# One build-time plan for gating, token mixing and the first channel chunk, with another matmul order

## The chip, the cores and the metric

The kernel runs on one core of one Trainium2 chip. The metric is the device time of one launch in microseconds (us), as the median of repeated runs. The engines are PE (TensorE, matmuls; PEld is its weight load), DVE (VectorE), ACT (ScalarE), POOL (GpSimd) and SP (SyncE, which here only issues DMAs). Each engine works through its own queue in program order.

## The reference

```python
attn_out = _attn_ref(q, k, v)            # 4 batches, 8 heads, 1152 keys, 576 pooled queries, 64 wide
x = attn_out.transpose(0, 2, 1, 3).reshape(4, 576, 512)
# gating (_moe_ref)
h = gelu(x @ w_in)                       # 512 -> 1024
u, v = h[..., :512], h[..., 512:]
v_n = (v - mean(v)) / sqrt(var(v) + 1e-6) * g_ln
v_s = einsum('ts,bsd->btd', w_sg, v_n) + b_sg[None, :, None]      # w_sg is 576 x 576
x = x + (u * v_s) @ w_out
# token mixing, then channel mixing (_moe2_ref)
u = x + (relu(x.T @ w_tok1) @ w_tok2).T  # 576 -> 256 -> 576 along tokens
out = u + relu(u @ w_ch1) @ w_ch2        # 512 -> 1536 -> 512
```

All weights arrive as 64-bit floats and are turned into pairs of 32-bit floats on the chip.

## The kernel before

Every matmul operand is held as a high and a low float32r part, and each product is three matmul passes (high by high, low by high, high by low). The state `xT` (channels on partitions, 2304 tokens) stays in SBUF through all stages.

Attention lays out its work with the class `Plan`: tasks with an engine, a duration, dependencies, rings of buffers and an urgency. `Plan.run` emits each engine's tasks in the order that this model gives; PE's order is written out in `line()`. Its last few tasks (the final part of the last head pair) are kept back in `rest` and emitted inside the next stage.

Gating, in `spatial`, runs batch by batch (b = 0 to 3). One batch is: V, five row tiles of `x @ w_in` for the v half (`v_mm`, L1001; four in odd batches, whose 64-row tail shares a tile with the batch before); O, the output product of the batch before (`wo_mm`, L1108, four tiles); U, four tiles of the u half (`u_mm`, L1067); S, four tiles of the product with `w_sg` (`sg_mm`, L1084). V and U results go through a gelu of two ACT and two DVE steps (L937 to L944). V is then normalised (L1014 to L1045) and split: the high part by ACT (L1051), the low part by POOL (`sub`, L241, tile `vn`). S results pass DVE (L1093), POOL (L1096), ACT (L1098) and DVE (L241, tile `g`) before O can read them. The input of the next batch is split by ACT (`x_high`, L399) and POOL (`x_low`, L241, tile `x`). V tiles of one pair, U, S and three of the four O tiles share three PSUM buffers (`ps2`).

Token mixing, in `mixing`, comes when the last O is done. For each batch: Y, five transposed tiles (`y_tr`, L1249, split by ACT L1251 and DVE L241); K, two tiles (`k1_mm`, L1266), with relu and split by ACT and DVE (`relu_split`, L1256 and L1257); H, four tiles (`k2_mm`, L1276), added to `xT` by DVE (L1280). Channel mixing follows in chunks of 512 tokens: C products (`c1`, L1332) alternate with D products (`c2`, L1356).

A weight is converted in pieces of 128 by 512 by class `Piece`: a load by SP, three DVE steps (L282, L289, L295), three ACT steps and a high part (L269, L275, L277, L305), and a low part on POOL (L241). In `spatial` and `mixing`, a `Feed` holds the pieces in order, and the table `HOOKS` says by hand at which places of the matmul code one further step of a piece (`c`), of the normalisation (`n`) or of the split of x (`x`) is emitted. Two blocks of `w_ch2` go out to DRAM and come back later; the other blocks of the mixing weights are converted where they are used: twelve of these pieces run during token mixing.

```python
def run(front, back, name, *a):
    r = front(*a, lambda: hook(name + "m"))
    hook(name + "a")
    for _ in back(*a, *r):
        hook(name + "e")
    hook(name + "z")
```

Of the kernel before, what the change touches and what calls it, by code (L numbers as in the profile page):

```python
# [30 lines left out]
YT = ((), (0, 1, 2), (3, 4), (), (), ())  # L31
HOOKS = {
# [21 lines left out]
}  # L54


class Plan:
# [28 lines left out]
    def run(self):  # L86
        free, order, mode = {}, [], None
# [62 lines left out]
def kernel(  # L150
# [184 lines left out]

    class Feed:


        def __init__(self):
            self.todo, self.ready, self.live = [], [], None  # L340
            self.added = self.done = 0

        def add(self, *todo):
            self.todo += todo
            self.added += len(todo)
            return self.added

        def load(self):
            while self.todo and len(self.ready) + (self.live is not None) < 2:
                self.ready.append(self.todo.pop(0))  # L350
                self.ready[-1].load(nc.sync)

        def steps(self, x):
            x.step1()
            x.early()
            x.signs()
            yield
            x.step2()
            yield
            x.step3()  # L360
            yield
            x.high()
            x.low_part()
            if x.away:
                for s in range(2):
                    x.send(s)

        def ops(self, n):
            for _ in range(n):
                self.load()  # L370
                if self.live is None:
                    if not self.ready:
                        return
                    self.live = self.steps(self.ready.pop(0))
                if next(self.live, 0) == 0:
                    self.live = None
                    self.done += 1
                    self.load()

        def until(self, count):  # L380
            while self.done < count:
                self.ops(1)

    feed = Feed()
# [21 lines left out]
    def attention():  # L406
# [493 lines left out]
        A.ws = far("aws", [P, NTT, T])  # L900
        A.c2 = [far(f"ac2{n}", [P, CC, 512]) for n in range(3)]
# [14 lines left out]
        for n in (1, 2):  # L916
            feed.add(*row_pieces(A.c2[n], w_ch2, 512 * n))
# [3 lines left out]
        for n, t in enumerate(order):  # L921
            if t["late"]:
                rest.append(t["fn"])
# [3 lines left out]

        def finish():
            yield lambda: [f() for f in rest[:-2]]
            yield lambda: [f() for f in rest[-2:]]  # L930
            yield lambda: a2.close()
        return finish()


# [12 lines left out]
    def spatial(fin):  # L947
        sr, sl = ExitStack(), ExitStack()
        mp = pool(ctx, "mid", 1, "right")
        W.append(block(mp, "w1"))  # L950
        JB = DTOK // P
        n0 = P * (T // P)

# [9 lines left out]
        wiv, wiu = W  # L963
        L = S0()
        L.gu = m1.tile([P, CC, T], F32, name="gu")
        L.XF = XF
        L.bank = lambda: ps2.tile([P, 2, 512], F32, tag="mm2", name="psz")

        def open_left():
            L.p = pool(sl, "wl", 1)  # L970
            L.ps = pool(sl, "psl", 1, space=PSUM)
            W.append(block(L.p, "wo"))
            L.wo = W[2]
            L.ws = [L.p.tile([P, NTT, T], F32R, name=f"wsg{s}") for s in range(2)]
            L.g = [L.p.tile([P, CC, T], F32R, name=f"g{s}") for s in range(2)]

        def bias_load():
            nc.sync.dma_start(out=b_bc, in_=b_sg.rearrange("(o t) -> o t", o=1).to_broadcast([P, T]))
            nc.sync.dma_start(out=g_half, in_=g_ln.rearrange("(c p) -> p c", p=P))
            g_scale(b_bc, b_bc, 0.5)  # L980
            g_scale(g_half, g_half, 0.5)

        PAIRS = ((0, 1), (2, 3), (4,))
        lst = {}

        def x_split(b, ti):
            x_high(b, ti)
            x_low(b, ti, nc.gpsimd)

        def v_mm(b, pi, mid):  # L990
            tis = PAIRS[pi]
            if pi == 0:
                lst[b] = m2.tile([P, NTT, 12], F32, tag="lst", name="lst")
                nc.gpsimd.memset(lst[b], 1.0)
            ps = ps2.tile([P, 2, 512], F32, tag="mm2", name="psv")
            for j, ti in enumerate(tis):
                t0 = TT[ti][0]
                if j == len(tis) - 1:
                    mid()
                for first, end, cc, sx, sw in products(range(CC)):  # L1000
                    nc.tensor.matmul(ps[:, j], X[sx][:, cc, t0:t0 + P], wiv[sw][:, cc], start=first, stop=end)  # L1001
            return (ps[:, 0:len(tis)],)

        def v_act(b, pi, ps):
            tis = PAIRS[pi]
            k_ = len(tis)
            sq = m3.tile([P, 2, DH], F32, tag="sq", name="sq")[:, 0:k_]
            gelu_front(ps, sq)
            yield
            gv = GV[:, tis[0]:tis[0] + k_]  # L1010
            gelu_back(gv, ps, sq)
            w = lst[b]
            for j, ti in enumerate(tis):
                nc.vector.bn_stats(w[:, ti, 0:6], gv[:, j])  # L1014
                nc.vector.bn_aggr(w[:, ti, 6:8], w[:, ti, 0:6])
# [4 lines left out]
        def v_norm(b):  # L1020

            w = lst[b]
            var, y, t_ = w[:, :, 8:9], w[:, :, 9:10], w[:, :, 10:11]

            def guess():

                nc.vector.tensor_scalar(
                    out=var, in0=w[:, :, 7:8], scalar1=4e-6, scalar2=None, op0=ALU.add)
                nc.vector.tensor_scalar(
# [180 lines left out]
    def mixing(L, fin):  # L1210
# [13 lines left out]
        for f in fin:  # L1224
            f()
# [210 lines left out]
```

## Time and profile before

| | before |
|---|---|
| median of 3 runs | 1160.88 us (1159.69 to 1162.37) |
| the profiled execution, its own time | 1162.66 us |
| its span, first to last instruction | 1160.8 us |
| PE busy | 1115.4 us (96%) |
| DVE busy | 656.9 us (57%) |
| ACT busy | 463.2 us (40%) |
| POOL busy | 575.3 us (50%) |
| mean granted TensorE clock | 0.988 |

The shares are means over stages with different limits. A busy PE here means that a matmul was under way, not that it ran at full rate: where the granted clock is below 1.00, part of the stretch ran at half of 2.4 GHz.

### The profile page before, as it was taken

The page shows a single profiled execution, that of the slowest core. Times are in us where ns is not written, and L with a number is a line of the kernel's source. Part 1 is how long each engine was busy: PE and PEld are TensorE (multiplying, and loading weights), DVE is VectorE, ACT ScalarE, POOL GpSimd, SP SyncE. Part 2 cuts the span into 40 slices and gives each one's busy share as a digit, 9 for nine tenths or more (in the row PEclk, how much of TensorE's full clock was granted, in tenths as well). Part 3 has the DMA queues.
Part 4 walks back from the last instruction along what each step waited for, and adds up shares of the span by engine and source line. Part 5 has one row for each costly group of instructions (what it writes and reads, how often), then busy time and mean ns, then how long its engine had stood idle before and what let it go on. Part 6 is the DMA issues. An engine that isn't in the chain of part 4 may idle for free.

```text
span 1160.8 us, 20808 instructions
## 1 busy us (share of the span) xinstructions
PE 1115.4 (96%) x8673; PEld 905.5 (78%) x8673; DVE 656.9 (57%) x888; ACT 463.2 (40%) x812; POOL 575.3 (50%) x405
## 2 busy tenths in 40 slices
PE   5999999999999999999799999979899999999998
PEld 4777777677777777777789898978788888888887
DVE  5777887877666788753757566778821211212121
ACT  2355555454444565544443433657511111111111
POOL 2688889888877788776263433542340202001000
PEclk9999999999999999999899999989999999999999
DMA  8122334234323443122430302132320000000000
GB/s 183 45 63 74 80 81 108 73 94 109 85 60 75 106 118 99 29 93 65 157 109 1 109 1 73 58 98 91 121 116 1 37 1 1 37 1 37 1 37 19
DMA packets 81966, 79.61 MB, mean 69 GB/s; under 512 B 42192, under 2 KB 67024, under 8 KB 80592
## 3 DMA queue, kind: packets, MB, share of 16 engines
q1 hardware_dynamic: 81872, 78.28, 23.6%
q8 instruction: 68, 1.11, 0.4%
q14 instruction: 26, 0.21, 0.1%
HBM read 62.51 MB, written 15.76 MB: 67 GB/s over the span
## 4 chain that ended last, share of the span: by engine, by line
PE 78%; DVE 9%; ACT 4%; POOL 4%; issue 3%; DMA 1%; SPq 0%; DVEq 0%; POOLq 0%; ACTq 0%
PE sT L599 14%; PE psc L1332 13%; PE po L1356 13%; PE po L622 13%; PE s L549 10%; PE psz L1108 3%; PE tt L498 2%; DVE mx L556 2%; PE psu L1067 2%; POOL gt L1096 2%; PE psv L1001 1%; PE psh L1276 1%; DVE wz L289 1%; PE pt L635 1%; PE pso L1108 1%
## 5 line engine op out<-in xcount | busy, mean ns | idle before, releaser
L613 POOL TENSOR_TENSOR acc<-acc,e 128x576 f32<-128x576 f32 x224 | 320.2, 1429 | 72.3 <-ACT e L607 59.3
L556 DVE TENSOR_REDUCE mx<-s 128x2 f32<-128x768 f32 (+1 forms) x240 | 215.3, 944 | 99.8 <-PE s L549 99.8
L607 ACT ACTIVATE e<-sT 128x576 f32<-128x576 f32 x288 | 169.8, 652 | 92.9 <-PE sT L599 90.6
L599 PE MATMUL sT<-q,k 64*128 64x288 f32 x1728 | 167.7, 305 | 0.2
L599 PEld LDWEIGHTS sT<-q,k 64*128 64x128 f32 x1728 | 129.4, 186 | 43.2 <-DVE mx L556 15.1
L622 PE MATMUL po<-e,vn 128*64 128x288 f32 x1152 | 161.5, 416 | 0.0
L1257 DVE SCALAR_TENSOR_TENSOR gc<-psc,gc 128x512 fp32r<-128x512 f32 (+1 forms) x50 | 34.0, 680 | 223.6 <-ACT gc L1256 223.6
L549 PE MATMUL s<-k,q 64*128 64x384 f32 (+1 forms) x1440 | 146.7, 344 | 2.9 <-ACT k L531 1.1
L1356 PE MATMUL po<-w,gc 128*128 128x512 f32 x588 | 144.6, 394 | 0.0
L1356 PEld LDWEIGHTS po<-w,gc 128*128 128x128 f32 x588 | 109.2, 188 | 23.3
L549 PEld LDWEIGHTS s<-k,q 64*128 64x128 f32 (+1 forms) x1440 | 111.1, 177 | 20.8 <-DVE mx L556 3.3
L1256 ACT ACTIVATE gc<-psc 128x512 fp32r<-128x512 f32 (+1 forms) x50 | 29.5, 589 | 232.9 <-PE psc L1332 232.9
L622 PEld LDWEIGHTS po<-e,vn 128*64 128x64 f32 x1152 | 74.5, 136 | 57.8 <-issue 17.6
L1332 PE MATMUL psc<-uc,w 128*128 128x512 f32 (+1 forms) x432 | 87.4, 355 | 0.0
L599 PE MATMUL sT<-nmT,pick 64*128 64x288 f32 x576 | 85.7, 293 | 0.0
L1332 PEld LDWEIGHTS psc<-uc,w 128*128 128x128 f32 x432 | 71.5, 188 | 12.2
L646 DVE RECIPROCAL pt<-pt 128x288 f32<-128x288 f32 x32 | 62.7, 1960 | 30.6 <-ACT pt L642 30.5
L1332 PE MATMUL psc<-x,w 128*128 128x512 f32 x288 | 70.7, 394 | 0.0
L1084 PE MATMUL pss<-wsg,vn 128*128 128x288 f32 x448 | 62.9, 302 | 5.0 <-POOL vn L241 4.5
L1084 PEld LDWEIGHTS pss<-wsg,vn 128*128 128x128 f32 x448 | 61.9, 195 | 5.7 <-POOL vn L241 5.0
L1332 PEld LDWEIGHTS psc<-x,w 128*128 128x128 f32 x288 | 54.0, 188 | 12.7
L237 POOL TENSOR_SCALAR uc<-xT 128x1024 fp32r<-128x1024 f32 x5 | 5.8, 1167 | 113.8 <-PE psc L1332 113.8
(113 smaller groups left out, 1551.8 us busy)
## 6 DMA issues: line engine op xcount, KB each, us to landing
ws<-in_moe_w_ch_dram SPq DMA_DIRECT2D x24, 512.0 KB, 3.5
qn<-in_q_dram SPq DMA_DIRECT2D x32, 288.0 KB, 4.9
kn<-in_k_dram SPq DMA_DIRECT2D x32, 288.0 KB, 4.2
vn<-in_v_dram SPq DMA_DIRECT2D x32, 288.0 KB, 3.5
out_dram<-ob SPq DMA_DIRECT2D x18, 256.0 KB, 2.0
ws<-in_moe_w_in_dram SPq DMA_DIRECT2D x8, 512.0 KB, 5.1
ac<-ws SPq DMA_DIRECT2D x16, 256.0 KB, 2.4
w<-ac SPq DMA_DIRECT2D x4, 1024.0 KB, 5.8
```

Source lines behind the costliest of these rows:

```text
L549: nc.tensor.matmul(ps[0:m, h, 0:KC], flat(c.q[x])[r, t * P:t * P + m], c.k[y][r, cs], start=(n == 0), stop=(n == 2))
L556: nc.vector.tensor_reduce(out=mx[i % 2][0:m, t, :, g], in_=ps[0:m, :, 0:KC], axis=AX.X, op=ALU.max, negate=True)
L599: nc.tensor.matmul(ps[:, h, 0:TC], left, right, start=(n == 0), stop=(n == 3))
L607: nc.scalar.activation(out=s.e[j], in_=ps[:, :, 0:TC], func=AF.Exp)
L613: eng.tensor_tensor(out=s.acc, in0=s.e[0] if j == 1 else s.acc, in1=s.e[j], op=ALU.add)
L622: nc.tensor.matmul(s.po[D * h:D * h + D, 0:TC], c.vn[:, h, j], s.e[j][:, h], start=(j == 0), stop=(j == J - 1))
L646: nc.vector.reciprocal(out=s.den, in_=s.den)
L1084: nc.tensor.matmul(ps[:, ch, 0:TC], V[sx][:, ti, db * P:(db + 1) * P], L.ws[sw][:, ti, ch * TC:(ch + 1) * TC], start=first, stop=end)
L1108: nc.tensor.matmul(ps[:, ch, 0:TC], L.wo[sw][:, db, cb * P:(cb + 1) * P], L.g[sx][:, db, ch * TC:(ch + 1) * TC], start=first, stop=end)
L1257: nc.vector.scalar_tensor_tensor(out=l_, in0=ps, scalar=0.0, in1=f32(h_), op0=ALU.max, op1=ALU.subtract)
L1332: nc.tensor.matmul(ps, WC1[f // 4][sw][:, cc, (f % 4) * P:(f % 4 + 1) * P], u[sx][:, cc], start=first, stop=end)
L1356: nc.tensor.matmul(pos[i, tt], g[i, f][sx][:, tt * P:(tt + 1) * P], WC2[f // 4][sw][:, f % 4], start=(f == 0 and n == 0), stop=(f == NF - ...
```

## The change

`HOOKS`, `Feed`, `spatial` and `mixing` go. One function, `later`, puts gating, token mixing and the first channel chunk into a second `Plan` as tasks, and emits them in the order that this plan gives. PE's order is again written by hand (`seq`); a new method `deadlines` works back from it to the latest start of every other task, and that is the task's urgency.

- PE order: in batch 0 V is five single tiles instead of pairs, and each S product of batch 0 is cut in two groups: P, which needs only high parts of the first four tiles, and the rest, S. In batch 3, Y and K of mixing batch 0 stand between S and O, and H, Y and K of neighbouring mixing batches are interleaved.
- Memory: token mixing uses the gating's tiles: `XF` and `V` hold Y, `W[0]` and `W[1]` hold the token weights and the first relu results. It opens no pools of its own but one for the second relu buffer; its PSUM is the gating's.
- Weights: `w_ch1`'s first block and all three blocks of `w_ch2` (16 pieces) are converted from batch 0's last U on, sent to DRAM and fetched later. The six token pieces follow when V and U of batch 3 free their weights, the second block of `w_ch1` after O of batch 3, and the third after the last H.
- Attention's plan and the channel chunks 1 to 4 keep their order and their work; some of their buffers lie elsewhere. No arithmetic is added or removed.

```diff
+FIRST = ((0,), (1,), (2,), (3,), (4,))
...
+    def deadlines(self):
+        line = sorted((t for t in self.tasks if "place" in t), key=lambda t: t["place"])
+        at, nominal, succ = 0.0, {}, {}
+        for t in line:
+            nominal[t["n"]] = at
+            at += t["dur"]
...
+        def latest(t):
+            if "latest" not in t:
+                ends = [latest(x) - lag for x, lag in succ.get(t["n"], ())]
+                t["latest"] = min([*ends, at]) - t["dur"] - t["land"]
+                if t["n"] in nominal:
+                    t["latest"] = min(t["latest"], nominal[t["n"]])
+                t["urgency"] += t["latest"]
+            return t["latest"]
...
-    class Feed:
...
+        got_b = plan.add("SP", 0.2, bias_load, begun=[left], land=4.0)
+        got_b = [plan.add("POOL", 0.9, lambda: (g_scale(b_bc, b_bc, 0.5),
+                                                 g_scale(g_half, g_half, 0.5)), after=[got_b])]
...
+        def conversion(x, home=(), begun=()):
+
+            a = plan.add("SP", 0.3, lambda: x.load(nc.sync), take=["ws"], begun=begun, land=4.0)
+            d1 = plan.add("DVE", 0.63, x.step1, after=[a], take=["wz"])
+            y = plan.add("ACT", 0.65, x.early, after=[a], take=["wy"])
+            e = plan.add("ACT", 1.25, x.signs, after=[a], take=["wd"])
+            d2 = plan.add("DVE", 0.9, x.step2, after=[d1, y], give=[("wy", y)])
+            d3 = plan.add("DVE", 0.88, x.step3, after=[d2, e],
+                          give=[("wd", e)] + ([] if x.away else [("ws", a)]))
+            h = plan.add("ACT", 0.62, x.high, after=[d3, *home])
+            l_ = plan.add("POOL", 1.4, x.low_part, after=[h], give=[("wz", d1)])
...
+        early = [(c, 0, s) for c in range(CC) for s in range(2)]
+        late = [(CC, 0, 0), (CC, 0, 1)] + [(c, 1, 0) for c in range(CC)]
...
+        held = [pe["U", 0, CC - 1]]
+        c10 = staged(col_pieces(A.c1, w_ch1, 0))
+        c2s = [staged(row_pieces(A.c2[n], w_ch2, 512 * n)) for n in range(3)]
...
+        y_home = [[rows(x) for x in XF], V]
...
+            if b == 0:
+                p, s_ = bl("P", 0), bl("S", 0)
+                seq(*p[:3], *s_[:2], p[3], *s_[2:])
+            elif b < B - 1:
+                seq(*bl("S", b))
...
+        seq(*S(3)[:2], Y(0)[0], S(3)[2], *Y(0)[1:], S(3)[3], *K(0),
+            *o[:2], Y(1)[0], o[2], Y(1)[1], o[3], Y(1)[2], *H(0)[:2])
+        for b in range(1, B):
+            y = Y(b + 1) if b + 1 < B else []
+            h = H(b - 1)[2:]
+            seq(K(b)[0], *y[:1], K(b)[1], *y[1:2], h[0], *y[2:], h[1], *H(b)[:2])
+        seq(*H(3)[2:])
+        for f in range(NF):
+            seq(("C", f))
+            if 4 <= f < 8:
+                seq(("T", f))
+            if f:
+                seq(("D", f - 1))
...
+        plan.sequence(line)
+        plan.deadlines()
+        for t in plan.run(free):
+            if t["fn"]:
+                t["fn"]()
```

## Rows read from the trace of the kernel before

**Rows 1.** Busy time by stage; after PEclk come DMA share and GB/s.
```profile
core 0: us, PE busy (x) PEld busy (x) DVE busy (x) ACT busy (x) POOL busy (x), PEclk, DMA share, GB/s
110.00:535.00 425.00, 423.01 (x4442) 312.61 (x4437) 311.23 (x368) 223.11 (x400) 353.48 (x241) 1.00 0.32 83
537.10:591.00 53.90, 47.32 (x287) 42.52 (x286) 32.84 (x55) 21.15 (x34) 21.43 (x18) 0.94 0.43 139
591.00:644.90 53.90, 51.80 (x354) 49.17 (x354) 35.10 (x57) 22.51 (x36) 21.98 (x18) 1.00 0.14 50
644.90:701.60 56.70, 54.76 (x366) 51.44 (x365) 37.45 (x62) 25.51 (x42) 24.64 (x21) 1.00 0.16 57
701.60:758.80 57.20, 53.45 (x354) 50.50 (x353) 37.99 (x63) 27.72 (x44) 23.66 (x18) 0.97 0.20 65
758.80:781.30 22.50, 14.76 (x98) 14.30 (x97) 17.67 (x25) 11.34 (x24) 9.23 (x9) 0.85 0.30 88
781.30:849.60 68.30, 64.20 (x386) 56.67 (x385) 55.38 (x80) 42.59 (x77) 23.00 (x16) 0.98 0.34 114
```

**Rows 2.** Waits of PE, 537.1 to 849.6: us in total, times, longest.
```profile
PE pso L1108 <- ACT g L1098: 7.7, 2, 3.9
PE psv L1001 <- ACT x L399: 4.5, 3, 2.1
PE pss L1084 <- POOL vn L241: 4.5, 2, 2.8
PE psh L1276 <- DVE r L1257: 3.0, 1, 3.0
PE psu L1067 <- DVE gv L944: 1.7, 2, 1.4
```

**Rows 3.** Timeline of PE: start, us, then engine, line, operation, tile, count.
```profile
542.80 1.68 PE L622 MATMUL po<-e,vn 128*64 128x288 f32 x12
...
544.89 8.46 PE L1001 MATMUL psv<-w,x 128*128 128x512 f32 x36
553.19 3.36 PE L1067 MATMUL psu<-x,w 128*128 128x288 f32 x24
...
686.82 14.99 PE L1084 MATMUL pss<-wsg,vn 128*128 128x288 f32 x112
701.64 8.35 PE L1001 MATMUL psv<-w,x 128*128 128x512 f32 x36
...
719.68 9.70 PE L1108 MATMUL psz<-g,wo 128*128 128x288 f32 x72
729.22 12.97 PE L1067 MATMUL psu<-x,w 128*128 128x288 f32 x96
742.02 1.22 PE L1084 MATMUL pss<-wsg,vn 128*128 128x288 f32 x8
...
781.30 2.62 PE L1249 MATMUL pty<-ident,xT 128*128 128x128 f32 x20
...
794.93 5.03 PE L1276 MATMUL psh<-x,r 128*128 128x288 f32 x36
799.80 6.72 PE L1266 MATMUL psr<-y,x 128*128 128x512 f32 x28
```

**Rows 4.** Timeline of POOL and DVE around the last K and H.
```profile
838.42 2.66 POOL L241 TENSOR_TENSOR uc<-xT,uc 128x1024 fp32r<-128x1024 f32 x1
...
838.98 2.65 DVE L295 SCALAR_TENSOR_TENSOR wz<-wz,wd 128x512 f32<-128x512 f32 x1
841.56 0.68 DVE L1257 SCALAR_TENSOR_TENSOR r<-psr,r 128x512 fp32r<-128x512 f32 x1
...
848.64 0.69 DVE L295 SCALAR_TENSOR_TENSOR wz<-wz,wd 128x512 f32<-128x512 f32 x1
```

**Rows 5.** Timeline of DVE: first step of the first token piece and last piece.
```profile
758.53 0.41 DVE L282 TENSOR_SCALAR wz<-ws 128x512 int32<-128x512 int32 x1
...
847.33 0.42 DVE L282 TENSOR_SCALAR wz<-ws 128x512 int32<-128x512 int32 x1
```

**Rows 6.** Timeline of POOL, the bias of batch 0.
```profile
563.42 0.68 POOL L237 TENSOR_SCALAR b_bc<-b_bc 128x576 f32<-128x576 f32 x1 [21.70 <-DMA b_bc<-in_moe_b_sg_dram]
```

More of the change, by code (lines that the diff above doesn't have):

```diff
@@ L97, in ready @@
                 at = max(at, d["end"] + (0.02 if d["eng"] == t["eng"] else self.LAG))
+            for d in t["begun"]:
+                if d["start"] is None:
+                    return None
+                at = max(at, d["start"])
             for ring in t["take"]:
@@ L334, in fetch @@
             nc.sync.dma_start(out=f32(to[s]), in_=x[s])
-    class Feed:
[L339 to L384, printed above, removed]
     XT = T + TAIL
@@ L926, in attention @@
         a1.close()
[L928 to L932, printed above, removed]
+        done = max(t["end"] for t in order if t["eng"] == "PE" and not t["late"])
+        free = {}
+        for t in order:
+            if not t["late"]:
+                free[t["eng"]] = max(free.get(t["eng"], 0.0), t["end"] - t["land"] - done)
+        free["SP"] = 0.0
+        return a2, rest, free
     def gelu_front(ps, sq):
@@ L962, in spatial @@
         GV = m1.tile([P, NTT, DM], F32, name="gv")
-        wiv, wiu = W
+        gu = m1.tile([P, CC, T], F32, name="gu")
         L = S0()
-        L.gu = m1.tile([P, CC, T], F32, name="gu")
-        L.XF = XF
-        L.bank = lambda: ps2.tile([P, 2, 512], F32, tag="mm2", name="psz")
-        def open_left():
[L970 to L975, printed above, removed]
+        plan = Plan()
@@ new lines, in later, with mm, big @@
+        for name, n in dict(mm=3, ml=1, sq=2, lst=2, ws=2, wd=1, wy=1, wz=2,
+                            c1=2, pu=2, g=2).items():
+            plan.ring(name, n)
+        pe, line, box = {}, [], {}
+        def mm(key, dur, fn, **kw):
+            pe[key] = plan.add("PE", dur, fn, **kw)
+        def big(key, ring="mm"):
+            p, tag = (ps2, "mm2") if ring == "mm" else (L.ps, "mm")
+            box[key] = p.tile([P, 2, 512], F32, tag=tag, name="ps" + key[0])
+            return box[key]
@@ new lines, in later @@
+        prev = None
+        for t in rest:
+            prev = plan.add(t["eng"], t["dur"], t["fn"], after=[prev])
+            if t["eng"] == "PE":
+                pe["rest", sum(k[0] == "rest" for k in pe)] = prev
+        def open_left():
+            a2.close()
+            p = pool(sl, "wl", 1)
+            L.ps = pool(sp, "psl", 1, space=PSUM)
+            L.wo = block(p, "wo")
+            L.ws = [p.tile([P, NTT, T], F32R, name=f"wsg{s}") for s in range(2)]
+            L.g = [p.tile([P, CC, T], F32R, name=f"g{s}") for s in range(2)]
@@ new lines, in fetch, with ws_load @@
+        def fetch(to, x, after=(), begun=(), land=9.0):
+            return [plan.add("SP", 1.0, lambda s=s: nc.sync.dma_start(out=f32(to()[s]), in_=x[s]),
+                             after=after[s] if after else (), begun=begun, land=land)
+                    for s in range(2)]
+        got_w1 = fetch(lambda: W[1], A.w1)
+        left = plan.add("SP", 0.05, open_left, begun=[prev])
+        def ws_load(s):
+            nc.sync.dma_start(out=f32(L.ws[s][:, 0:CC]), in_=A.ws[s][:, 0:CC])
+            for r in range(0, P, TAIL):
+                nc.sync.dma_start(
+                    out=f32(L.ws[s][r:r + TAIL, CC:NTT]), in_=A.ws[s][0:TAIL, CC:NTT])
@@ L977, in bias_load @@
+        got_ws = [plan.add("SP", 1.5, lambda s=s: ws_load(s), begun=[left], land=9.0)
+                  for s in range(2)]
         def bias_load():
@@ L990, in v_mm, with x_tasks @@
-        def v_mm(b, pi, mid):
-            tis = PAIRS[pi]
-            if pi == 0:
+        def x_tasks(b):
+            for ti in range(NTT):
+                n = 1 if ti < CC else 0.75 if b % 2 else 1.5
+                h = plan.add("ACT", 0.6 * n, lambda b=b, ti=ti: x_high(b, ti), after=[pe["U", b - 1, CC - 1]])
+                l_ = plan.add("POOL", 1.36 * n, lambda b=b, ti=ti: x_low(b, ti, nc.gpsimd), after=[h])
+                x_of[b, ti] = [h, l_]
+        def v_mm(b, ti):
+            tis = next(x for x in VP[b] if ti in x)
+            j = ti - tis[0]
+            ps = box["V", b, tis[0]] if j else big(("V", b, ti))
+            t0 = TT[ti][0]
+            for first, end, cc, sx, sw in products(range(CC)):
+                nc.tensor.matmul(ps[:, j], X[sx][:, cc, t0:t0 + P], wiv[sw][:, cc], start=first, stop=end)
@@ L993, in v_mm, with v_tasks, start @@
+        def v_tasks(b):
+            def start(b=b):
                 lst[b] = m2.tile([P, NTT, 12], F32, tag="lst", name="lst")
                 nc.gpsimd.memset(lst[b], 1.0)
[L995 to L1015, printed above, removed]
+            ms = plan.add("POOL", 0.15, start, take=["lst"])
@@ new lines, in v_tasks @@
+            for t0, t1 in NORMS[b] if b in NORMS else ((0, len(bns)),):
+                nm = plan.add("DVE", 2.1, lambda t0=t0, t1=t1: norm(b, t0, t1), after=bns[t0:t1])
+                for ti in range(t0, t1):
+                    ap_of[b, ti] = plan.add("DVE", 0.71, lambda ti=ti: apply(b, ti), after=[nm],
+                                            give=[("lst", ms)])
+            for ti in range(NTT):
+                n = 1.0 if ti < CC else 0.9
+                h = plan.add("ACT", 0.62 * n, lambda ti=ti: v_high(b, ti),
+                             after=[ap_of[b - (ti == CC and b % 2), ti], pe.get(("S", b - 1, CC - 1))])
+                l_ = plan.add("POOL", 1.36 * n, lambda ti=ti: v_low(b, ti), after=[h])
+                sp_of[b, ti] = [h, l_]
@@ new lines, in add_xt, with o_tasks @@
+            nc.vector.tensor_tensor(out=xs, in0=box[key][:, :, 0:TC], in1=xs, op=ALU.add)
+        def o_tasks(b):
+            for cb in range(CC):
+                ring = "mm" if cb else "ml"
+                mm(("O", b, cb), 3.2, lambda cb=cb: wo_mm(b, cb),
+                   after=[*(got_wo if b == 0 else ()), *sum((s34[b, db] for db in range(CC)), [])],
+                   take=[ring])
+                o_of[b, cb] = plan.add(
+                    "DVE", 0.75, lambda cb=cb: add_xt(("O", b, cb), b, cb), after=[pe["O", b, cb]],
+                    give=[(ring, pe["O", b, cb])])
@@ new lines, in later, with rows @@
+        todo.append(Piece(w_tok1[n0:T].rearrange("(a p) n -> p a n", p=TAIL), tail_dst))
+        got_k1 = sum(here(todo, [pe["V", B - 1, CC - 1]], pe["V", B - 1, 2]), ())
+        todo = []
+        for j in range(3):
+            c = slice(j * (T // 3), (j + 1) * (T // 3))
+            todo.append(Piece(w_tok2[:, c].rearrange("(a p) n -> p a n", p=P), dst(wk2, c)))
+        got_k2 = sum(here(todo, [pe["U", B - 1, CC - 1]], pe["U", B - 1, 2]), ())
+        def rows(x):
+            return x.rearrange("p (a n) -> p a n", n=DM)
@@ L1276, in k2_mm, with k2_tasks @@
                     nc.tensor.matmul(
-                        ps[:, ch, 0:TC], c.r[sx][:, jb, cb * P:(cb + 1) * P],
+                        ps[:, ch, 0:TC], r[sx][jb][:, cb * P:(cb + 1) * P],
                         wk2[sw][:, jb, ch * TC:(ch + 1) * TC], start=first, stop=end)
-            xs = two(xT[:, cb, b * T:(b + 1) * T])
-            nc.vector.tensor_tensor(out=xs, in0=ps[:, :, 0:TC], in1=xs, op=ALU.add)
+        def k2_tasks(b):
+            for cb in range(CC):
+                mm(("H", b, cb), 1.62, lambda cb=cb: k2_mm(b, cb),
+                   after=[*(got_k2 if b == 0 else ()), *sum((k_of[b, jb] for jb in range(JB)), [])],
+                   take=["mm"])
+                h_of[b, cb] = plan.add(
+                    "DVE", 0.75, lambda cb=cb: add_xt(("H", b, cb), b, cb), after=[pe["H", b, cb]],
+                    give=[("mm", pe["H", b, cb])])
@@ new lines, in open_weights @@
+        def open_weights():
+            sl.close()
+            p = pool(ctx, "wc", 1)
+            for i in range(3):
+                W.append(block(p, f"wc{i}"))
+            p = pool(sk, "rp", 1)
+            r = [p.tile([P, JB, DM], F32R, name=f"r{s}") for s in range(2)]
+            r_home.append([[x[:, jb] for jb in range(JB)] for x in r])
+        wopen = plan.add("SP", 0.05, open_weights, begun=[pe["O", B - 1, CC - 1]])
+        for b in range(B):
+            y_tasks(b)
+            k1_tasks(b)
+            k2_tasks(b)
@@ L1403 @@
         make_identity(nc, ident)
-        mixing(*spatial(attention()))
+        later(*attention())
 _INS = ['q', 'k', 'v', 'moe_w_in', 'moe_g_ln', 'moe_w_sg', 'moe_b_sg', 'moe_w_out',
```

600 lines of the change are left out of this document (331 added, 269 removed), and 21 rows, old and new, of the table HOOKS.

## Prediction

> **What bounds the kernel now.** I read the page first: PE is busy nearly throughout, so only time in which PE stands still or runs at half clock can be won without removing work. The table by stage then tells where that is [rows 1]. In attention, 110 to 535 us, PE is busy 423.0 of 425.0 us: 2.0 us lost, in a stretch laid out by the same kind of plan that this change extends, with DVE busy 73% of it (311.23 of 425). From 537.1 (first V) to 849.6 (first C of channel mixing) the rows add up to 286.2 us of PE in 312.5 us, so 26.3 us stand idle, and in four of the six stages the granted clock is below 1.00: 0.94, 0.97, 0.85 and 0.98. After 849.6 PE's order and work stay as they are, so I count nothing there.
>
> The waits of PE name the idle places [rows 2]: 7.7 us in two waits of the last O for ACT's `g`; 4.5 us of V for the next batch's `x`; 4.5 us of S for POOL's `vn`; 3.0 us of the last H for DVE's `r`; 1.7 us of U for DVE's gelu of V (its PSUM buffer).
>
> To include the slow clock I rebuild the stretch from starts on the timeline in places with neither [rows 3]. V: (553.19 - 544.89) / 3 = 2.77 us a tile. S: (701.64 - 686.82) / 4 = 3.71. O: (729.22 - 719.68) / 3 = 3.18. U: (742.02 - 729.22) / 4 = 3.20. H: (799.80 - 794.93) / 3 = 1.62; its row says 5.03, so a duration includes 0.16 of overlap. K: (6.72 - 0.16) / 2 = 3.28. Y: 2.6 for five tiles. Attention's left-over matmuls inside V: 544.89 - 542.80 = 2.1. By stage, work against time [rows 1]:
>
> - batch 0: 5 x 2.77 + 2.1 + 12.8 + 14.8 = 43.6 of 53.9, loss 10.3
> - batch 1: 4 x 2.77 + 12.7 + 12.8 + 14.8 = 51.4 of 53.9, loss 2.5
> - batch 2: 54.2 of 56.7, loss 2.5
> - batch 3: 51.4 of 57.2, loss 5.8
> - last O: 12.7 of 22.5, loss 9.8
> - token mixing: 8 x 3.28 + 16 x 1.62 + 4 x 2.6 = 62.5 of 68.3, loss 5.8
>
> That is 36.7 us of loss against 275.8 us of work. This 36.7 is the most that the change can give.
>
> **The change part by part.** Attention's tasks and order are the same, and so are the matmuls of channel mixing: nothing before 537.1 or after 849.6 moves but by shift. No PE work is added; S of batch 0 in two groups is the same 28 matmuls a tile. So the sum is of losses that go or stay.
>
> *Last O, 9.8 us.* S ends, and O needs `g`, which passes DVE, POOL, ACT and DVE. In the new order K of mixing batch 0 stands there: 6.6 us of matmuls. The chain's steps are about 0.8, 1.7, 0.7 and 0.9 us by the plan's own figures; with hand-offs under 5 us. The cover is enough by 1.5 us, and O follows in one run. What is late next is Y's split before K, with the last S tile between them (3.7 us against two steps of about 1.2). I leave 0.3 us. If a converted piece sits in DVE's queue at the wrong moment, some 2.6 us come back, as in the last H below.
>
> *Batch 0, 10.3 us.* Three things. Singles instead of pairs let DVE start on V after 2.8 us of matmuls, not 5.5, which takes the U waits of 1.7 us and more; P needs only high parts, so that the five low parts on POOL are covered by three P tiles (3 x 2.1 us), and the longest wait of 2.8 us [rows 2] goes; with the pauses the half clock goes (0.94 [rows 1]). What stays is the chain from the last V through the gelu, one normalisation for all five tiles and four high parts to P, covered by the 12.8 us of U, with U's own gelus on the same two engines. I find it just covered and leave 2.5 us (bounds 0.5 to 6). One added wait: the plan lets the bias land after 4 us and puts its scaling on POOL by that; in the trace it ran at 563.42, after POOL had been waiting for that DMA [rows 6]. Behind it in POOL's queue stand the low parts of `vn`. Even at 563.4 + 0.9 + 5 x 1.4 = 571.3 they meet the first S at about 572, so it costs nothing, with under 1 us to spare.
>
> *Batches 1 to 3, 10.8 us.* The hand table put the splits of `x` where V reaches the tile before them (4.5 us), and in batch 3 pieces ahead of `vn` on POOL (1.7 of the 4.5 us, plus clock). The plan knows when V, U and S need each split. S covers 14.8 us, in which POOL has about 7 us of `x`, 6.6 us of gating and some pieces at 1.4 us: it fits, the last tiles of `x` being due only 8 us into V. I leave 0.7, 0.7 and 1.0.
>
> *Token mixing, 5.8 us.* In the last H a piece's step on DVE stood in front of `r` for 2.65 us [rows 4], and PE waited 3.0 us [rows 2] and ran at half clock after. Now two H tiles of the batch before (3.2 us) stand between K and its H, and twelve pieces no longer fall into this stretch: at most four to six do. I leave 1.5.
>
> *Pieces moved.* There are 30 before and after. Sixteen instead of eight go through DRAM: 4 MB more written and 4 MB more read, on queues busy 14% to 43% in these stages [rows 1]; hidden. The loads come on SP's queue behind sends that wait for POOL's low part, as the plan has it; a late send delays later loads, and so the weights of C and D, not the gating. Eight pieces at some 2.4 us of DVE move out of token mixing into the gating, where DVE has 36% free (143 of 222 us busy); four go into the first channel chunk, where it is idle. Cover gone, the price is rival C.
>
> The row of 2.65 us deserves a word, because the plan reckons with fixed durations. That step takes 0.69 us elsewhere [rows 4], and here it ended 0.55 us after POOL's `uc` at 841.08: DVE stood until POOL was done. The Trainium skill, page SBUF — State Buffer, section Who interferes with whom, says that a DVE instruction with two SBUF inputs contends with a GpSimd instruction that reads SBUF, and whoever comes second blocks fully; the trace agrees. By that rule the moved steps would meet a POOL busy 41% of the gating instead of 34% of mixing, so eight pieces of three steps at 7% more hits of about 1 us would add some 1.7 us of DVE time, which the sum by rows leaves out as off the path.
>
> Left in all: 2.5 + 0.7 + 0.7 + 1.0 + 0.3 + 1.5 = 6.7 us, for 277 us of work. Attention's 2.0 us in 425 is the kinder bound (1.3 us here); I take the larger, since here PE has three PSUM buffers for tiles of 3 us and more chains. Gain 36.7 - 6.7 = 30.0 us. The profiled execution took 1162.66, so its like would take 1132.7; the median of the runs lies 1.8 below it, which makes 1130.9. I say 1131.
>
> **The rivals.**
>
> *A, half the gain.* DVE becomes the pace of the gating. Its rows from 537.1 to 849.6 add up to 216.4 us; less four pieces that is 206 in 282 us, 73%. For it: DVE works in order, steps stretch when POOL is busy [rows 4], and the plan's order is fixed by mean durations, so each of some twelve hand-overs (V to U, U to S, S to V, K to H) could lose 1 to 2 us, and half clock follows a pause as in batch 0. Against it: attention ran at just that share with 2.0 us lost [rows 1]. Price: 15 us of 36.7 stay beside my 6.7, so 1146; range 1139 to 1156.
>
> *B, no change.* The waits return elsewhere in the same sum: 1158.6 to 1163.2. For it only that every chain is as long as before. Against: the two largest losses are filled with matmuls that wait for nothing new.
>
> *C, slower.* The weights of the first channel chunk come too late. 26 pieces must be through before C uses them, between the last U of batch 0 (about 563) and the first C (about 819): 9.8 us each. Token mixing ran them at (847.33 - 758.53) / 17 = 5.2 us [rows 5], which speaks against it. But they go last in urgency, hold one of two buffers until the sends land, and compete with the gating. Each microsecond over 9.8 makes C 26 us late; at 11.0 the gain is used up, and at 12 us the time is 1131 + 57 = 1188.
>
> **How the numbers follow.** Forecast 0.66 (1124 to 1139), A 0.24, B 0.04, C 0.06. The predicted time is the forecast's. Below stands the full loss gone, 1124; above, A's middle, 1146: 0.66 plus a good half of A is 8 in 10. A measurement can tell about 0.2% (2.3 us) from no change. Faster by more than that: 0.66 + 0.24 and a little of B, 0.91; within it 0.03; slower 0.06.
>
> **What would show it.** Right: the first V again at about 537 and the first C at about 819, 282 us later; no PE wait of over 1.5 us between S of batch 3, K and O; the granted clock at 1.00 in all these stages but batch 0; the row of waits of O for `g` gone; C and D without a wait for weights. Wrong step by step: P waits for ACT's high part or S for POOL (batch 0 mis-sized); V waits for `x` (batches 1 to 3); H waits for `r` (mixing); many waits of 0.5 to 2 us for DVE (A); C, D or K waits for a DMA or for a weight's low part (C).

## The result and the profile after

The changed kernel takes 1140.61 us (median of four runs, 1140.52 to 1140.8) against 1161.62 us for the kernel before on the same chip: ratio 0.9819, 95% interval 0.98 to 0.9837. It is faster by 21.0 us, clear of the noise; 30 were forecast, and 1140.6 lies in the range of 1124 to 1146.

Busy time by stage of the kernel after, with the columns of [rows 1]; the stretches begin with the first V, the V of batches 1 to 3, the K of mixing batch 0, the K of mixing batch 1 and the first C:

```profile
536.10:581.00 44.90, 44.46 (x286) 39.82 (x285) 38.04 (x60) 23.70 (x41) 23.66 (x22) 1.00 0.45 155
581.00:632.30 51.30, 51.30 (x354) 49.38 (x353) 39.99 (x58) 24.98 (x41) 26.13 (x20) 1.00 0.25 73
632.30:686.30 54.00, 54.00 (x366) 51.63 (x365) 45.48 (x68) 28.61 (x47) 26.29 (x19) 1.00 0.22 79
686.30:740.60 54.30, 53.73 (x374) 51.55 (x373) 45.05 (x66) 28.36 (x45) 24.97 (x18) 1.00 0.23 76
740.60:765.10 24.50, 24.50 (x171) 23.36 (x170) 18.87 (x27) 13.04 (x23) 7.27 (x6) 1.00 0.32 100
765.10:825.30 60.20, 48.93 (x294) 43.80 (x293) 36.86 (x47) 24.39 (x39) 15.01 (x10) 0.91 0.49 163
825.30:1139.00 313.70, 309.62 (x1442) 253.56 (x1440) 58.15 (x91) 51.91 (x95) 30.55 (x19) 1.00 0.10 35
```

Five stages now have PE busy almost to the end, at a granted clock of 1.00, where four of six stood below it [rows 1]. One stage has not: 765.1 to 825.3, with 11.3 us of idle PE and a clock of 0.91. The waits of PE from 530 to 900 us of the kernel after say what that is:

```profile
PE psH L1335 <- DVE x L257: 9.9, 1, 9.9
PE psS L1157 <- DVE gt L1183: 0.6, 1, 0.6
PE psK L1311 <- DVE r L1304: 0.5, 1, 0.5
PE psK L1311 <- DVE w L1304: 0.5, 1, 0.5
PE psS L1157 <- DVE gu L1085: 0.4, 1, 0.4
PE psH L1335 <- DVE vn L257: 0.3, 1, 0.3
PE po L1446 <- ACT gc L1301: 0.2, 1, 0.2
```

All waits of [rows 2] are gone, and one of 9.9 us has come: an H that waits for DVE. The timeline of the kernel after, leading up to that H at 786.21, shows where DVE was (rows of SP, DVE, ACT and PE, others left out):

```profile
761.67 2.07 SPq L960 DMA_DIRECT2D wc<-ac  x4
...
763.79 1.67 SPq L327 DMA_DIRECT2D ac<-ws  x3
...
770.46 1.23 DVE L257 TENSOR_TENSOR x<-psY,x 128x1024 fp32r<-128x1024 f32 x1 [0.60 <-ACT x L1294]
773.28 1.04 PE L1278 MATMUL psY<-ident,xT 128*128 128x128 f32 x8
...
777.70 10.73 SPq L277 DMA_DIRECT2D ws<-in_moe_w_ch_dram  x4
781.34 0.66 ACT L285 ACTIVATE wy<-ws 128x512 int32<-128x512 uint32 x1 [10.91 <-DMA ws<-in_moe_w_ch_dram]
781.41 0.43 DVE L298 TENSOR_SCALAR wz<-ws 128x512 int32<-128x512 int32 x1 [9.72 <-DMA ws<-in_moe_w_ch_dram]
...
783.59 1.00 ACT L1294 CAST x<-psY 128x1024 fp32r<-128x1024 f32 x1
783.73 0.69 DVE L1304 SCALAR_TENSOR_TENSOR r<-psK,r 128x512 fp32r<-128x512 f32 x1 [1.00 <-ACT r L1301]
...
784.93 1.22 DVE L257 TENSOR_TENSOR x<-psY,x 128x1024 fp32r<-128x1024 f32 x1
...
786.21 0.85 PE L1335 MATMUL psH<-w,w 128*128 128x288 f32 x2 [9.86 <-DVE x L257]
...
789.25 3.59 PE L1335 MATMUL psH<-w,r 128*128 128x288 f32 x24
```

Read it from the bottom. The H at 786.21 is the last one of batch 0. Its inputs, the token weights and batch 0's relu (both in tiles named `w`), were there long before; what it lacks is a PSUM buffer. H and Y take turns on three of them, and the next one in turn still holds Y tiles of batch 2 (773.28), until ACT has copied their high part (783.59) and DVE has taken the low part (784.93). The two H of batch 1 behind it (789.25) also need `r`, the relu of a K (783.73). In both engines' queues these steps stand behind the first step of a weight piece, at which DVE sat 9.72 us (781.41) and ACT 10.91 us (781.34) until its load had landed. That load was issued at 777.70 and not before, because its buffer still held an earlier piece, whose sends to DRAM had gone out at 763.79, just behind four fetches of 1 MB each. The DMA issues of 761.6 to 778, with the median time from issue to landing, close the chain:

```profile
wc<-ac SPq DMA_DIRECT2D x4, 1024.0 KB, 9.5
ac<-ws SPq DMA_DIRECT2D x3, 256.0 KB, 13.8
ws<-in_moe_w_ch_dram SPq DMA_DIRECT2D x1, 512.0 KB, 3.6
```

A send of 256 KB took 13.8 us to land. The plan reckons with 3.5 us for a send and 9 us for a fetch, each as if it were alone.

### The profile page after: what moved, and what is told of

It is laid out like the page before. It is cut to its first block, busy times and chain, and to the rows that moved or that the text cites. A ratio compares the mean times of both kernels' runs of the same rounds, so it can differ in the third digit from the quotient of the medians.

```text
span 1139.0 us, 20880 instructions
## 1 busy us (share of the span) xinstructions
PE 1107.9 (97%) x8673; PEld 900.7 (79%) x8673; DVE 671.2 (59%) x884; ACT 464.7 (41%) x808; POOL 579.7 (51%) x405
## 4 chain that ended last, share of the span: by engine, by line
PE 87%; DVE 5%; DMA 5%; issue 1%; SPq 1%; ACT 1%; POOL 0%; POOLq 0%; DVEq 0%; ACTq 0%
PE sT L565 15%; PE po L588 13%; PE po L1446 13%; PE psc L1416 12%; PE s L515 11%; PE psO L1206 4%; PE psS L1157 4%; PE psV L1028 4%; PE psU L1128 3%; DMA ac<-ws 2%; DMA ws<-in_moe_w_ch_dram 2%; PE tt L464 2%; DVE mx L522 2%; PE pt L601 1%; PE psK L1311 1%
## 5 line engine op out<-in xcount | busy, mean ns | idle before, releaser
L1446 PE MATMUL po<-wc,gc 128*128 128x512 f32 x408 | 100.4, 394 | 0.4 <-ACT gc L1301 0.2
L1446 PEld LDWEIGHTS po<-wc,gc 128*128 128x128 f32 x408 | 76.1, 188 | 19.0 <-DVE gc L1304 1.1
L1157 PE MATMUL psS<-wsg,vn 128*128 128x288 f32 x448 | 60.9, 295 | 1.0 <-DVE gt L1183 0.6
L1157 PEld LDWEIGHTS psS<-wsg,vn 128*128 128x128 f32 x448 | 59.7, 188 | 1.6 <-DVE gt L1183 0.8
L1416 PE MATMUL psc<-x,wc 128*128 128x512 f32 (+1 forms) x288 | 59.1, 357 | 0.0
L579 POOL TENSOR_TENSOR acc<-e 128x576 f32<-128x576 f32 x32 | 47.8, 1493 | 20.2 <-ACT e L573 20.2
L257 POOL TENSOR_TENSOR vn<-gv,vn 128x512 fp32r<-128x512 f32 (+1 forms) x20 | 28.5, 1448 | 56.3 <-ACT vn L1118 56.0
L1416 PEld LDWEIGHTS psc<-x,wc 128*128 128x128 f32 x288 | 47.8, 188 | 8.8
L565 PEld LDWEIGHTS sT<-nmT,pick 64*128 64x128 f32 x576 | 54.5, 185 | 0.0
```

What stands on the lines that cost most here:

```text
L565: nc.tensor.matmul(ps[:, h, 0:TC], left, right, start=(n == 0), stop=(n == 3))
L579: eng.tensor_tensor(out=s.acc, in0=s.e[0] if j == 1 else s.acc, in1=s.e[j], op=ALU.add)
L1157: nc.tensor.matmul(ps[:, ch, 0:TC], V[sx][:, ti, db * P:(db + 1) * P], L.ws[sw][:, ti, ch * TC:(ch + 1) * TC], start=first, stop=end)
L1416: nc.tensor.matmul(ps, W[WC1[f // 4]][sw][:, cc, (f % 4) * P:(f % 4 + 1) * P], u[sx][:, cc], start=first, stop=end)
L1446: nc.tensor.matmul(pos[i, tt], g[i, f][sx][:, tt * P:(tt + 1) * P], W[WC2[f // 4]][sw][:, f % 4], start=(f == 0 and n == 0), stop=(f == NF ...
```

## The experiments

Theory Q: the sends, and then the load, are late because 4 MB of fetches go first; DVE and ACT, which take their work in order, stand at the missing piece, with the steps that H needs behind it. (The expectations name the relu there; by the rows above, the PSUM buffer that Y's split frees came first.) Theory D: that stretch has too much work for DVE, whatever the transfers do.

**late**: the four fetches held back, so that SP issues the sends and the next loads ahead of them.

```diff
-got_c1 = [fetch(lambda: W[2], A.c1, after=c10, begun=[wopen]), [], []]
-got_c2 = [fetch(lambda: W[3], A.c2[0], after=c2s[0], begun=[wopen]),
+got_c1 = [fetch(lambda: W[2], A.c1, after=c10, begun=[pe["H", 1, CC - 1]]), [], []]
+got_c2 = [fetch(lambda: W[3], A.c2[0], after=c2s[0], begun=[pe["H", 2, 1]]),
```

> The four 1 MB fetches of the first channel weights go to SP's queue behind the three sends and the load of the next piece (held until H of mixing batches 1 and 2), nothing else. Theory Q (the sends and then the load stand behind 4 MB of fetches in the DMA queue; the buffer comes free late, the next piece's first step blocks DVE's and ACT's queues, and the relu behind it keeps H waiting): the sends land in about 3 us instead of 13.8, PE's wait of 9.9 us before H falls below 1 us, and with the half clock after it (3.5 us at half rate) the time falls by 9.9 + 1.7 to about 1129. Theory D (DVE has too much in that stretch, whatever the transfers do): a wait of 5 us or more stays, 1136 or more.

1130.82 us (1129.25 to 1131.84), ratio to the kernel before 0.9735 (0.9713 to 0.9756). PE's waits in this kernel from 530 to 900 us:

```profile
PE psH L1335 <- DVE x L257: 1.5, 1, 1.5
...
```

And its DMA issues of 745 to 800 us:

```profile
ac<-ws SPq DMA_DIRECT2D x4, 256.0 KB, 2.5
```

The sends (`ac<-ws`) land in 2.5 us, the wait of 9.9 us is 1.5 us, and the time falls by 9.8 us. As theory Q had it, but for the 1.5 us. What is left of the wait is DVE's own work: from 774.04, when K's second tile is done, to 778.26, when H gets its buffer, DVE is busy without a gap with two relus, two splits of Y and the first steps of two pieces.

**half**: only the second of the two lines above is changed; two fetches stay ahead.

```diff
-got_c2 = [fetch(lambda: W[3], A.c2[0], after=c2s[0], begun=[wopen]),
+got_c2 = [fetch(lambda: W[3], A.c2[0], after=c2s[0], begun=[pe["H", 2, 1]]),
```

> Only two of the four fetches stay ahead of the sends (2 MB). Theory Q: at the 380 GB/s or so of that stretch 2 MB less is 5.3 us less, so the wait falls from 9.9 to about 4.6 us and the time to 1134 to 1136. Theory D: no change beyond 2 us, 1138 to 1141.

1138.86 us (1137.71 to 1139.24). The time is the one that theory D gave (1138 to 1141) and misses theory Q's (1134 to 1136). The wait, 7.8 us, now of K, fits neither number.

```profile
PE psK L1311 <- DVE r L1304: 7.8, 1, 7.8
...
```

The timeline of this kernel shows that it is still a load that DVE waits for, which theory D does not have:

```profile
762.02 1.13 SPq L327 DMA_DIRECT2D ac<-ws  x2
771.58 0.38 SPq L277 DMA_DIRECT2D ws<-in_moe_w_ch_dram  x1
...
775.64 0.43 DVE L298 TENSOR_SCALAR wz<-ws 128x512 int32<-128x512 int32 x1 [10.09 <-DMA ws<-in_moe_w_ch_dram]
```

With 2 MB ahead the load could go 9.6 us after the sends (771.58 - 762.02), against 13.9 us with 4 MB (777.70 - 763.79): the transfers do shrink with the burst. But the plan also drew the piece forward, ahead of the first of K's two relus, for which K's second tile already waits, so that PE had less to do in the meantime. The dose is not clean in this run. Every variant is planned anew, so an edit to the fetches can also move steps on DVE and ACT. In `late` too a piece stands ahead of that relu, but there DVE waits for no load between 760 and 786 us.

**more**: the block for D fetched twice, as extra work that changes no result.

```diff
+fetch(lambda: W[3], A.c2[0], after=c2s[0], begun=[wopen])
 got_c2 = [fetch(lambda: W[3], A.c2[0], after=c2s[0], begun=[wopen]),
```

> The block of w_ch2 is fetched twice, so that 6 MB stand ahead of the last sends and the load instead of 4; the second fetch is extra work that changes no result. Theory Q: 5.3 us more, a wait of about 15 us, 1145 to 1147. Theory D: 1140 to 1142.

1146.44 us (1144.77 to 1147.97).

```profile
PE psH L1335 <- DVE x L257: 15.4, 1, 15.4
...
```

The number is theory Q's, though its way is another: the second fetch of a tile waits on SP until the first has landed (the two went out at 772.13 and 775.87), and the last sends and the load (776.88, landed 9.0 us later) stand behind it in SP's queue. So this is no clean dose of transfers either; it shows again that a later load makes H wait longer.

**actq**: the four fetches at the same place in the plan, issued by ACT.

```diff
+def afetch(to, x, after=(), begun=()):
+    return [plan.add("ACT", 0.1, lambda s=s: nc.scalar.dma_start(out=f32(to()[s]), in_=x[s]),
+                     after=after[s], begun=begun, land=9.0) for s in range(2)]
...
-got_c1 = [fetch(lambda: W[2], A.c1, after=c10, begun=[wopen]), [], []]
-got_c2 = [fetch(lambda: W[3], A.c2[0], after=c2s[0], begun=[wopen]),
+got_c1 = [afetch(lambda: W[2], A.c1, after=c10, begun=[wopen]), [], []]
+got_c2 = [afetch(lambda: W[3], A.c2[0], after=c2s[0], begun=[wopen]),
```

> The same four fetches at the same place, but issued from ACT's queue instead of SP's. Theory Q, if it is the order within one queue that holds the sends back: the sends land in about 3 us, the wait falls below 2 us, about 1130. Theory Q, if it is the share of the 16 DMA engines: the sends still take 6 us or more, a wait of 3 to 8 us, 1134 to 1139. Theory D: 1138 to 1142.

1137.07 us (1136.07 to 1137.63), a wait of H of 6.5 us. Another queue takes only part of it away. The median of the four sends is 5.3 us, but the last of them, on the chain to H, took 9.9 us to land, and DVE still got its next pieces late:

```profile
PE psH L1339 <- DVE x L257: 6.5, 1, 6.5
...
764.84 9.86 DMA ac<-ws
...
777.85 0.43 DVE L298 TENSOR_SCALAR wz<-ws 128x512 int32<-128x512 int32 x1 [4.39 <-DMA ws<-in_moe_w_ch_dram]
```

So it is both the order within a queue and the engines that all queues share, whose busy share was 0.99 to 1.03 from 764 to 776 us of this kernel. The Trainium skill, page Trainium Kernel Development and Optimization, section Key Constraints, says that DMAs from SP's, ACT's and POOL's queues run on the same 16 engines and interleave; the run agrees, with 6.5 us of wait left from 9.9.

**late_olast**: `late`, with Y and K back behind the last O.

```diff
-seq(*S(3)[:2], Y(0)[0], S(3)[2], *Y(0)[1:], S(3)[3], *K(0),
-    *o[:2], Y(1)[0], o[2], Y(1)[1], o[3], Y(1)[2], *H(0)[:2])
+seq(*S(3), *o, *Y(0), *K(0), *Y(1), *H(0)[:2])
```

> From the kernel with the late fetches (1130.8): Y and K of mixing batch 0 go back behind the last O, so that nothing stands between S of batch 3 and O. Theory K (the matmuls of K and Y are what covers the chain from S to O): a wait of 4 to 5 us of O for its split input comes back, and half clock with it, 1136 to 1138. Theory P (the loss of 9.8 us was the pieces in DVE's and ACT's queues, and these have left the place anyway): a wait under 2 us, 1130 to 1132.

1142.16 us (1141.18 to 1145.1), 11.3 us more than `late`. (This run and the next three were on another chip than `late`; the kernel before took 1161.62 us there against 1160.52, so their distances to `late` can be off by about 1 us.)

```profile
PE psO L1206 <- ACT g L1192: 3.8, 2, 3.6
PE psH L1335 <- DVE vn L257: 2.8, 2, 2.1
PE psY L1278 <- DVE w L1304: 2.1, 1, 2.1
PE po L1446 <- ACT gc L1301: 1.8, 1, 1.8
PE psH L1335 <- DVE x L257: 1.7, 1, 1.7
PE psK L1311 <- DVE x L257: 1.1, 1, 1.1
```

The O wait comes back at about half its old 7.7 us [rows 2]. It is not the chain alone: the last S is done at 736.4, but its step on DVE stood behind two steps of a weight piece until 738.2, and only the 3.1 us from there to O (741.3) are DVE, POOL and ACT in turn. So the pieces had not left the place, as theory P supposed. Most of the rest lies in Y, K and H, which now follow each other with nothing between. In the profiled execution, the highest of the four, the stretch from the first V to the first C is 13.1 us longer than in `late` (291.7 against 278.6). Theory K holds, with a share of pieces in the O wait. The time is above both theories: the order of PE is worth more than its expectation gave it.

**late_nop**: `late`, with S of batch 0 whole.

```diff
-if b == 0:
+if False:
     mm(("P", b, db), 2.13, lambda db=db: sg_mm(b, db, 0),
...
-p, s_ = bl("P", 0), bl("S", 0)
-seq(*p[:3], *s_[:2], p[3], *s_[2:])
+seq(*bl("S", 0))
```

> From the kernel with the late fetches (1130.8): S of batch 0 is whole again, four tiles of 28 matmuls that need high and low parts. Theory: S waits 3 to 6 us for POOL's low parts, 1134 to 1138. Rival (the order by deadlines brings the low parts early enough by itself): under 1 us, 1130 to 1132.

1136.52 us (1134.35 to 1136.93), 5.7 us more. The profiled execution was the lowest of the four; in it S waits 1.5 us and 0.2 us at its start, and a D waits longer:

```profile
PE po L1446 <- ACT gc L1301: 2.2, 2, 1.8
PE psS L1157 <- issue: 1.5, 1, 1.5
...
PE psS L1157 <- POOL vn L257: 0.2, 1, 0.2
```

The time is in the theory's range, but the wait is not: 1.5 us of it are put down to no engine ("issue") and 0.2 us to POOL, where 3 to 6 us were expected. (POOL works on the five low parts until 568.8 meanwhile, so it may be behind the 1.5 us too.) From the first V to the first V of batch 1 the kernel takes 46.3 us, `late` 44.9 and the kernel before 53.9. So the direct worth of P is 1 to 2 us. The profiled execution is 2.5 us longer than that of `late` in all, 1.7 of it behind the first C; what makes up the rest of the 5.7 us does not show in it.

**late_pairs**: `late`, with V of batch 0 in pairs.

```diff
-VP = [FIRST, PAIRS[:2], PAIRS, PAIRS[:2]]
+VP = [PAIRS, PAIRS[:2], PAIRS, PAIRS[:2]]
```

> From the kernel with the late fetches (1130.8): V of batch 0 in pairs as before. Theory (singles let DVE begin 2.8 us earlier and free PSUM buffers one by one): U waits 1 to 3 us for a buffer or P for its high parts, 1132 to 1134. Rival: nothing, 1130 to 1131.5.

1132.49 us (1129.81 to 1133.79). In its profiled execution no U and no P waits, and S waits 0.2 us for POOL. The difference to `late` is within what the two runs scatter, so the times leave it open. In the profiles batch 0 takes 46.2 us against 44.9, with a wait of 1.0 us of S for DVE's `gt`, and the stretch from the first V to the first C no more than in `late` (278.3 against 278.6). The waits of U that singles were to take away do not come back with pairs.

**dmaplan_late**: `late`, with the plan told that transfers share one path.

```diff
-def fetch(to, x, after=(), begun=(), land=9.0):
-    return [plan.add("SP", 1.0, lambda s=s: nc.sync.dma_start(out=f32(to()[s]), in_=x[s]),
+def fetch(to, x, after=(), begun=(), land=6.0):
+    return [plan.add("SP", 2.7, lambda s=s: nc.sync.dma_start(out=f32(to()[s]), in_=x[s]),
...
-a = plan.add("SP", 0.3, lambda: x.load(nc.sync), take=["ws"], begun=begun, land=4.0)
+a = plan.add("SP", 1.4, lambda: x.load(nc.sync), take=["ws"], begun=begun, land=2.6)
...
-return [plan.add("SP", 0.1, lambda s=s: x.send(s), after=[(h, l_)[s]], land=3.5,
+return [plan.add("SP", 0.7, lambda s=s: x.send(s), after=[(h, l_)[s]], land=2.5,
```

> From the kernel with the late fetches (1130.8): the plan is told that transfers share one path (SP is taken for 2.7 us by a fetch of 1 MB, 1.4 by a load, 0.7 by a send, with shorter landings). Theory (what is left of PE's waits, 1.5 us before H and some 2.5 us in the first channel chunk, comes from DVE and ACT waiting in order for loads that the plan thinks landed): 1127 to 1130. Rival (those losses are DVE's own): 1130 to 1132.

1137.38 us (1135.57 to 1138.56), slower by 6.6 us, where faster was expected. An H waits 5.9 us for DVE, and this time no engine waits for a transfer there (775 to 805 us). That wait, and POOL and DVE of this kernel just before that H at 799.31:

```profile
PE psH L1335 <- DVE vn L257: 5.9, 1, 5.9
...
792.36 1.57 DVE L298 TENSOR_SCALAR wz<-ws 128x512 int32<-128x512 int32 x1
...
794.04 1.34 DVE L305 SCALAR_TENSOR_TENSOR wz<-wz,wy 128x512 int32<-128x512 int32 x1
794.92 2.65 POOL L257 TENSOR_TENSOR x<-xT,x 128x1024 fp32r<-128x1024 f32 x1
795.48 2.64 DVE L311 SCALAR_TENSOR_TENSOR wz<-wz,wd 128x512 f32<-128x512 f32 x1
...
798.04 1.21 DVE L257 TENSOR_TENSOR vn<-psY,vn 128x1024 fp32r<-128x1024 f32 x1
```

It is the 2.65 us of [rows 4] again: the piece's last step starts inside POOL's split of the first chunk and ends 0.55 us after it (798.12 against 797.57), with the split of Y that frees H's PSUM buffer (798.04) behind it. The piece's other two steps meet POOL's work too. The three take 5.55 us here and 1.80 us at 784 to 787 us of the same kernel, so the meeting makes up 3.7 of the 5.9 us at most; the rest is what else stands in DVE's queue. The new figures for the DMAs set the pieces at a place where this meeting happens, which a plan with fixed durations does not see. Behind the first C the expectation did come true: from there to the end this kernel takes 312.5 us, `late` 314.1.

**late_all** and **late_again**: `late`, with the four later fetches held too, and `late` once more on the same chip.

```diff
-fetch(lambda: W[0], A.c2[1], after=[x + [pe["H", B - 2, CC - 1]] for x in c2s[1]]),
-fetch(lambda: W[5], A.c2[2], after=c2s[2], begun=[copen])]
+[],
+[]]
...
+            if f == 3:
+                got_c2[1] = fetch(lambda: W[0], A.c2[1], after=c2s[1], begun=[pe["C", 1]])
+            if f == 7:
+                got_c2[2] = fetch(lambda: W[5], A.c2[2], after=c2s[2], begun=[pe["C", 5]])
```

> From the kernel with the late fetches (1130.8): the other four fetches of 1 MB are held as well, those of w_ch2's second block until C(1) and of its third block until C(5) of the first chunk, so that the sends and loads of the last pieces go first there too. Theory Q: D no longer waits for a relu that stands behind a late load, and the 2.5 us that the first chunk takes above a later one go, 1127.5 to 1129.5. Rival (the first chunk's loss comes from the pieces' own steps): 1130 to 1131.5.

> The kernel with the late fetches once more, on the same chip as the one before it, so that the two can be compared: 1130 to 1132 by both theories.

`late_all`: 1128.05 us (1127.57 to 1130.95), ratio 0.971 (0.9694 to 0.9727). `late_again`: 1130.41 us (1129.41 to 1132.11), ratio 0.9729 (0.9713 to 0.9745). The wait of D for `gc`, the relu of C that it reads, is gone in `late_all`, whose C and D run at one step of 2.80 us from the first on (first two rows), where a D of `late_again` waited 1.1 us and took 3.28 us (last two rows):

```profile
822.30 2.96 PE L1446 MATMUL po<-wc,gc 128*128 128x512 f32 x12
825.10 2.96 PE L1416 MATMUL psc<-x,wc 128*128 128x512 f32 x12
...
825.55 3.44 PE L1446 MATMUL po<-wc,gc 128*128 128x512 f32 x12 [1.13 <-ACT gc L1301]
828.83 2.96 PE L1416 MATMUL psc<-x,wc 128*128 128x512 f32 x12
```

From the first C to the end `late_all` takes 312.5 us and `late_again` 314.8; up to there, from the first V, both take 278.4. So the mechanism shows in the profile, at its expected 2.3 us. The medians differ by 2.4 us, but the two intervals overlap: the first V stands at 538.3 in one profile and at 534.7 in the other, behind the same attention, and this scatter is larger than the gain. Both kernels beat the change: `late` by 9.8 us, `late_all` by 12.6.

## Why the prediction was right, and where it was not

**Work, loss and place.** The work was counted right, the loss that stays was not. The first V stands at 536.12 and the first C at 825.33: 289.2 us, against 275.8 us of work as counted. So 13.4 us of loss are left of 36.7, not 6.7. (The prediction's 277 us of work is a slip for its own 275.8, and its rows of PE add up to 286.3, not 286.2; the sum of losses does not use either.)

**Batch 0.** Forecast 2.5 us left, measured 1.4 (44.95 us from V to V, 43.6 of work). The U waits are gone and P never waits, but not for the reasons given. Without P batch 0 takes 1.4 us longer than in `late`. With pairs it takes 1.2 us longer, and even then no U waits. Of the 8.9 us that batch 0 became shorter, the two edits to PE's order that the prediction named for it show under 3. The rest must have come from what else changed there, such as the order of the other engines' work; no run undid that, or both edits at once.

**Batches 1 to 3.** Forecast 2.4 us left, measured 0.3 in batch 3 and none in the other two: 51.3, 54.0 and 54.3 us against 51.4, 54.2 and 54.0 of work, the last with Y of batch 0 in it. No V waits for `x` any more. This was not undone by itself: that the earlier splits are the cause is read from the waits that went, not tried.

**Last O.** Forecast 0.3 us left, measured none. `late_olast` confirms the cover, and more of it than was reckoned: 11.3 us, with what Y, K and H lose in it.

**Rival A.** Fell. DVE is busy 38.0 to 45.5 us of each batch of the gating, up to 85% (38.04 of 44.90), and PE lost next to nothing there. A high share alone did not make DVE the pace.

**Where it failed.** The step is in *Pieces moved*: "a late send delays later loads, and so the weights of C and D, not the gating". A late load delays the engine, not only the piece: DVE and ACT take their work in order, and whatever stands behind the piece's first step waits with it. So *Token mixing*, of which 1.5 us were to stay, lost 12.7 us (63.5 us from the first H to the first C for 50.8 of work): 9.9 in one wait, and half of the 3.5 us of matmuls at half clock behind it. The granted clock fell to 0.50 (1.2 GHz) some 3 us into the wait and was back 3.5 us after its end, as in this stretch of 2 us (columns of [rows 1]):

```profile
786.00:788.00 2.00, 1.79 (x7) 1.79 (x8) 1.93 (x4) 1.34 (x3) 1.28 (x1) 0.50 0.00 0
```

The sign that the prediction gave for a fault in mixing, "H waits for `r`", was near but not it: H waited for the PSUM buffer that a split of Y frees. What stands behind the first C, counted as unchanged, lost 2.5 us (313.7 against 311.2 from there to the end), 2.2 of it in the first channel chunk. The prediction also read the four fetches as "hidden" by the mean share of the queues in [rows 1]; the mean said nothing of four in a row with a 256 KB send behind them. `late` and `late_all` take most of both losses away by moving four fetches and then eight, with no other edit: 278.6 us instead of 289.2 to the first C, and 312.5 instead of 313.7 behind it. Some 2.8 and 1.3 us stay.

**Where luck came in.** The forecast's own band was 1124 to 1139. 1140.6 lies above it, and in the range only because the range went up to the middle of rival A, whose cause was not there. And the fault was larger than the miss. In the profiles mixing and what follows the first C cost 13.7 us more than forecast, while the other stages cost 5.5 us less: batch 0 1.1, batches 1 to 3 2.4, the last O 1.0, and the first V stood 1.0 earlier. Without these the time would have stood at the upper edge of the range, near 1146. Once the fetches are moved, the stretch to the first C is shorter than forecast (278.6 against 282.5).

**Rival C** named late loads as the danger, but as a pace of 9.8 us for all pieces and with the price on C. The pace was no problem; one load at one place was.

**Lock between DVE and POOL.** It was put at 1.7 us of DVE time off the path. In the change it cost PE nothing that the waits show; in `dmaplan_late` three such steps in a row made up as much as 3.7 us of a wait of 5.9 us, because the step that frees H's buffer stood behind them.

What stays open: what won most of batch 0, and why `late_nop` costs 5.7 us by its median and 2.5 by its profiled execution (its lowest run against the highest of `late`). A third buffer for the pieces, which would tell the buffer's part of the stall from the transfer's, was not tried.

## What to carry to other kernels

When background work shares an in-order engine with the chain that feeds the matmuls, ask of its first step not how long it takes but what it waits for: one load that lands 10 us late holds up everything queued behind it. A plan with a fixed landing time per transfer was wrong here just where large fetches were issued in a row; put small transfers that free a buffer ahead of large ones that nobody needs yet. And fill the gap of a dependent chain with another stage's matmuls: that, with the order of Y, K and H that goes with it, was worth 11.3 us here, more than either edit to the first batch of the gating.

## What the runs showed of the hardware

A send of 256 KB landed in 2.5 us (median, `late`) with no fetch ahead of it and in 13.8 us behind four fetches of 1 MB in the same queue; with the fetches on ACT's queue the slowest of four took 9.9 us and the median was 5.3 us. DVE at 85% of a stretch, beside POOL at 53% (23.66 of 44.90), cost PE a wait of 0.4 us there.
